# Retention and channel mix on one core: k transposed by whole 128x128 products, mu transposed on chip, and a rewritten order of all pieces

## The chip, the core and the metric

The kernel runs on one core of a Trainium2 chip. A core has TensorE (PE, the matrix engine; PEld is its weight load), VectorE (DVE), ScalarE (ACT), GpSimd (POOL) and SyncE (SP), each with its own instruction stream executed in order, and 16 DMA engines that they share. The metric is the device time of the program in microseconds, as the median of several runs.

## The reference

Per batch b and head h a state of 64x64 is decayed and updated at each of 768 tokens, read by q, and the result x goes through a channel mix with the token before it.

```python
# B=4, H=8, S=768, D=64;  d_model = 512, d_ff = 1024
gamma = 1 - 2.0 ** (-5.0 - arange(H));  scale = 1 / sqrt(D)
for t in range(S):
    state = gamma * state + k[t]^T v[t]            # per batch and head
    y[t]  = scale * q[t] @ state
x = y with heads side by side                      # (B, S, 512)
xk = mu_k * x + (1 - mu_k) * x_prev                # x_prev: the token before, zero at t = 0
xr = mu_r * x + (1 - mu_r) * x_prev
out = sigmoid(xr @ w_r) * (relu(xk @ w_k) ** 2 @ w_v)
```

## The kernel before

The work is cut into 12 blocks of 256 tokens (three for each batch, `more(n)` is false for the last of a batch). Inside a block the 256 tokens are two halves (u = 0, 1) of 128; each partition holds two neighbouring tokens (i = 0, 1), so that partitions 0 to 63 hold half 0 and 64 to 127 half 1. Head pairs (j, with hp = 0, 1 inside the pair) are processed by 64x64 products that use the array in four quarters.

All scheduling is by hand: the string `ORDER` (lines 16 to 63) lists all pieces, and each engine executes its own pieces in that order. A word such as `K.3.1@5` is a code, the block, further arguments, and the PSUM bank after the @. The codes are:

- `lk`, `lq`, `lv`: loads of k, q and v of a block. `lk.n` is issued by SP, `lk.n.2` by POOL; q and v by POOL. `wk`, `wr`, `wv`: weight loads by POOL. `mu`: the two mu vectors, by ACT.
- `ks`: `scale_k` (line 181), k times its decay, on DVE (`ks.n.0`) or POOL (`ks.n.1`).
- `T.n.0`, `T.n.1`: `trans` (line 195), transposes of q and of the scaled k on PE, 32 products of 64x64 each; both share two PSUM banks. `E.n.0`, `E.n.1`: `transed` (line 207), the copies to SBUF by ACT.
- `S`: `scores` (line 222, PE); `M`: `masked` (line 234, DVE). `C`: `state` (line 244, PE); `U`: `summed` (line 262, DVE); `G`: `decayed` (line 272, POOL). `I`: `inter` (line 278) and `Y`: `intra` (line 290), both PE. `D`: `yout` (line 310, DVE), which writes x transposed.
- `dx`: `differ` (line 318), x minus its predecessor, on DVE in blocks 0 and 1 and on POOL after that. `X.n.w.j.j+1`: `mixed` (line 325, DVE), xk for w = 0 and xr for w = 1, in four pieces each.
- `K`: `keys` (line 334, PE), four groups; `Q`: `squared` (line 344, ACT). `R`: `gate` (line 351, PE); `s`: `opened` (line 358, ACT). `V`: `values` (line 363, PE), in halves of the contraction; `O`: `result` (line 370, DVE); `st`: `store` (line 376, SP).
- `z.n`: `zeros` (line 397), n products of zeros on PE which nobody reads.

Attention pieces run ahead of the channel mix pieces by one or two blocks, and from the third block on the order interleaves them with K, R and V. The buffers are rings (`ring`): 4 for q, v and k as loaded, 3 for the scaled k.

Of the kernel before, what the change touches and what calls it, by code (L numbers as in the profile page):

```python
# [9 lines left out]
F16 = mybir.dt.float16  # L10
# [4 lines left out]
KSC = 64.0  # L15
ORDER = """
lk.0 lq.0 lv.0 gy lk.1.2 lq.1 lv.1 wk.0 ks.0.0 wk.1 z.13@0 T.0.0@01 wr T.0.1 lk.2.2 E.0.0 C.0@23
U.0.0 lq.2 E.0.1 z.1@4 I.0.0@45 U.0.1 G.0.1 z.2@6 S.0.0@01 mu S.0.1@23 lv.2 ks.1.0 z.2@7 T.1.0@67
wv.0 M.0.1 T.1.1 E.1.0 M.0.0 C.1@23 wv.1 E.1.1 U.1.0 Y.0 G.1.0 S.1.0@67 D.0 I.1.0@01 lk.3.2 M.1.0
z.2@2 S.1.1@45 M.1.1 lq.3 dx.0.0 Y.1 X.0.0.0.1 X.0.0.1.2 X.0.0.2.3 lv.3 X.0.0.3.4 X.0.1.0.1 z.9@2  # L20
K.0.0@2 X.0.1.1.2 X.0.1.2.3 K.0.2@4 X.0.1.3.4 lk.4.2 Q.0.0 U.1.1 D.1 R.0.0@5 ks.2.1 Q.0.2 T.2.0@23
R.0.1@4 s.0.0 lq.4 dx.1.0 T.2.1 s.0.1 K.0.1@5 E.2.0 lv.4 X.1.0.2.3 C.2@4 X.1.0.1.2 K.0.3@0 E.2.1
X.1.0.3.4 X.1.0.0.1 Q.0.1 X.1.1.0.1 S.2.0@23 K.1.0@1 G.1.1 M.2.0 Q.0.3 lq.5 V.0.0.0@5 U.2.0 Q.1.0
X.1.1.3.4 V.0.1.0@4 X.1.1.2.3 X.1.1.1.2 lk.5.2 V.0.1.1 G.2.0 V.0.0.1 O.0.1 ks.3.1 I.2.0@01 st.0.1
O.0.0 S.2.1@23 R.1.0@4 M.2.1 st.0.0 T.3.0@67 s.1.0 lv.5 T.3.1 lk.7 Y.2 E.3.0 lq.6 C.3@45 D.2
R.1.1@2 E.3.1 lv.6 K.1.1@3 U.3.0 s.1.1 ks.4.1 U.3.1 S.3.0@67 Q.1.1 I.3.0@45 S.3.1@01 M.3.0 K.1.2@2
G.3.1 lk.8 V.1.1.0@3 M.3.1 Q.1.2 dx.2.1 V.1.0.0@2 K.1.3@0 lk.6.2 X.2.0.3.4 C.4@67 Q.1.3 X.2.0.0.1
Y.3 X.2.0.1.2 lq.7 T.4.0@01 X.2.0.2.3 T.4.1 V.1.0.1 U.4.0 ks.5.1 E.4.0 D.3 V.1.1.1 E.4.1 O.1.0
K.2.0@6 G.4.0 O.1.1 st.1.0 lk.9 ks.7.1 S.4.0@01 U.4.1 Q.2.0 I.4.0@23 st.1.1 S.4.1@45 M.4.0 K.2.1@7
K.2.2@6 M.4.1 G.4.1 Q.2.1 lk.11 dx.3.1 K.2.3@7 Q.2.2 V.2.0.0@4 Q.2.3 V.2.1.0@5 lv.7 X.2.1.2.3  # L30
X.2.1.3.4 V.2.0.1 X.2.1.1.2 lq.8 X.3.1.0.1 X.3.0.0.1 V.2.1.1 X.2.1.0.1 X.3.0.2.3 R.2.0@7 X.3.0.3.4
X.3.0.1.2 R.2.1@6 X.3.1.1.2 s.2.0 X.3.1.2.3 T.5.0@01 X.3.1.3.4 s.2.1 T.5.1 O.2.0 ks.6.1 C.5@7
E.5.0 Y.4 U.5.0 st.2.0 O.2.1 R.3.0@4 E.5.1 D.4 st.2.1 G.5.0 K.3.0@5 lk.10 s.3.0 ks.8.1 S.5.0@23
Q.3.0 I.5.0@01 S.5.1@67 M.5.0 R.3.1@4 dx.4.1 K.3.1@5 M.5.1 s.3.1 K.3.2@4 Q.3.1 K.3.3@5 lv.8
X.4.0.0.1 Q.3.2 X.4.0.3.4 V.3.0.0@6 X.4.0.1.2 lq.9 X.4.0.2.3 Q.3.3 X.4.1.1.2 V.3.1.0@7 X.4.1.0.1
X.4.1.3.4 V.3.0.1 X.4.1.2.3 V.3.1.1 O.3.0 C.6@45 st.3.0 O.3.1 T.6.0@23 T.6.1 U.6.0 lq.10 Y.5
st.3.1 E.6.0 U.6.1 K.4.0@4 D.5 ks.9.1 E.6.1 R.4.0@5 Q.4.0 S.6.0@23 G.6.1 I.6.0@01 S.6.1@67 M.6.0
R.4.1@4 s.4.0 dx.5.1 K.4.1@5 M.6.1 s.4.1 K.4.2@4 Q.4.1 lv.9 X.5.0.2.3 X.5.0.1.2 K.4.3@5 X.5.0.0.1
Q.4.2 X.5.0.3.4 V.4.0.0@6 X.5.1.0.1 Q.4.3 X.5.1.1.2 V.4.1.0@7 X.5.1.2.3 X.5.1.3.4 V.4.0.1 V.4.1.1
O.4.0 T.7.0@45 st.4.0 O.4.1 T.7.1 lq.11 C.7@23 E.7.0 Y.6 st.4.1 U.7.0 K.5.0@7 G.7.0 D.6 E.7.1  # L40
ks.10.1 R.5.0@2 U.7.1 Q.5.0 S.7.0@45 I.7.0@67 S.7.1@01 M.7.0 s.5.0 K.5.1@3 G.7.1 dx.6.1 K.5.2@2
M.7.1 Q.5.1 K.5.3@3 Q.5.2 lv.10 X.6.0.0.1 V.5.0.0@0 X.6.0.1.2 Q.5.3 X.6.0.3.4 V.5.1.0@1 X.6.0.2.3
X.6.1.3.4 V.5.0.1 X.6.1.2.3 X.6.1.1.2 V.5.1.1 X.6.1.0.1 O.5.0 R.5.1@3 st.5.0 C.8@0 s.5.1 T.8.0@45
U.8.0 T.8.1 Y.7 O.5.1 G.8.0 E.8.0 R.6.0@0 ks.11.1 st.5.1 D.7 E.8.1 K.6.0@1 s.6.0 S.8.0@45 dx.7.1
Q.6.0 I.8.0@67 S.8.1@23 M.8.0 R.6.1@0 K.6.1@1 M.8.1 s.6.1 lv.11 K.6.2@0 Q.6.1 X.7.0.0.1 X.7.0.1.2
K.6.3@1 X.7.0.2.3 Q.6.2 X.7.0.3.4 V.6.0.0@2 X.7.1.0.1 X.7.1.2.3 Q.6.3 V.6.1.0@3 X.7.1.3.4
X.7.1.1.2 V.6.0.1 V.6.1.1 O.6.0 C.9@01 st.6.0 O.6.1 T.9.0@45 T.9.1 U.9.0 Y.8 st.6.1 E.9.0 U.9.1
K.7.0@0 D.8 G.9.1 E.9.1 R.7.0@1 dx.8.1 Q.7.0 S.9.0@45 I.9.0@67 S.9.1@23 M.9.0 R.7.1@0 s.7.0
K.7.1@1 M.9.1 s.7.1 K.7.3@0 Q.7.1 X.8.0.1.2 X.8.0.3.4 K.7.2@1 X.8.0.2.3 Q.7.3 X.8.0.0.1 V.7.0.0@2
X.8.1.1.2 Q.7.2 X.8.1.0.1 V.7.1.0@3 X.8.1.3.4 X.8.1.2.3 V.7.0.1 V.7.1.1 O.7.0 C.10@01 st.7.0 O.7.1  # L50
T.10.0@45 T.10.1 U.10.0 Y.9 st.7.1 E.10.0 G.10.0 K.8.1@0 D.9 E.10.1 R.8.0@3 U.10.1 dx.9.1 Q.8.1
S.10.0@45 I.10.0@67 S.10.1@01 M.10.0 K.8.0@2 s.8.0 G.10.1 R.8.1@3 M.10.1 Q.8.0 K.8.2@2 X.9.0.0.1
s.8.1 X.9.0.1.2 V.8.0.0@0 X.9.0.2.3 Q.8.2 X.9.0.3.4 V.8.1.0@1 X.9.1.0.1 X.9.1.1.2 K.8.3@2
X.9.1.2.3 X.9.1.3.4 C.11@3 Q.8.3 T.11.0@45 U.11.0 T.11.1 Y.10 G.11.0 E.11.0 V.8.0.1 D.10 E.11.1
V.8.1.1 O.8.0 dx.10.1 S.11.0@45 O.8.1 st.8.0 I.11.0@67 S.11.1@23 R.9.0@0 M.11.1 st.8.1 K.9.2@1
s.9.0 M.11.0 K.9.1@0 Q.9.2 X.10.0.0.1 R.9.1@1 X.10.0.1.2 Q.9.1 X.10.0.2.3 K.9.0@4 X.10.0.3.4
X.10.1.1.2 s.9.1 K.9.3@5 X.10.1.2.3 Q.9.0 X.10.1.3.4 X.10.1.0.1 Y.11 Q.9.3 V.9.0.0@4 D.11 V.9.0.1
dx.11.1 V.9.1.0@5 O.9.0 V.9.1.1 st.9.0 X.11.0.0.1 K.10.0@4 X.11.0.1.2 X.11.0.3.4 R.10.0@6
X.11.0.2.3 Q.10.0 X.11.1.0.1 K.10.1@4 X.11.1.3.4 s.10.0 X.11.1.1.2 K.10.2@7 X.11.1.2.3 Q.10.1
O.9.1 R.10.1@6 st.9.1 Q.10.2 V.10.0.0@5 s.10.1 V.10.1.0@4 K.10.3@6 R.11.0@7 Q.10.3 K.11.0@6 s.11.0  # L60
V.10.0.1 Q.11.0 V.10.1.1 O.10.0 R.11.1@6 st.10.0 O.10.1 K.11.1@7 st.10.1 s.11.1 K.11.2@6 Q.11.1
K.11.3@7 Q.11.2 V.11.1.0@4 Q.11.3 V.11.0.0@5 V.11.0.1 V.11.1.1 O.11.0 st.11.0 O.11.1 st.11.1
# [4 lines left out]
def kernel(  # L67
# [32 lines left out]
    gk_np = gam[None, :, None] ** (C - 1 - tok[:, None, :])  # L100
# [5 lines left out]
        [x.reshape(P, -1) for x in (gk_np, gd_np, g0_np, pw_np)], axis=1  # L106
# [15 lines left out]
    KS = ring("ks_", 3, [H, 2 * D], F16)  # L122
    QT = ring("qT_", 3, [2, NJ, C], F16)
    KT = ring("kT_", 3, [2, NJ, 2, D], F16)
# [11 lines left out]
    csm = const.tile([P, 2 * H + (2 + LOG) * NJ], F32, name="csm_sb")  # L136
    gy = const.tile([P, NJ, C], F32, name="gy_sb")
    zero = const.tile([P, 512], F16, name="zero")
    muk = const.tile([P, NCO], F32, name="muk")
    mur = const.tile([P, NCO], F32, name="mur")  # L140
# [7 lines left out]
    gk = csm[:, 0:o]  # L148
    gd = csm[:, o : o + NJ]
    g0 = csm[:, o + NJ : o + 2 * NJ]  # L150
    pw = csm[:, o + 2 * NJ :].rearrange("p (l j) -> p l j", l=LOG)
# [4 lines left out]
    relus = iter(range(NFO * NBLK))  # L156
# [24 lines left out]
    def scale_k(n, e, j0=0, j1=NJ):  # L181
        h0, h1 = 2 * j0, 2 * j1
        (nc.vector, nc.gpsimd)[e].tensor_tensor(  # L183
            out=KS(n)[:, h0:h1].rearrange("p h (i d) -> p (h i) d", i=2),
            in0=K32(n)[:, h0:h1].rearrange("p h (i d) -> p (h i) d", i=2),
            in1=gk[:, 2 * h0 : 2 * h1, None].to_broadcast([P, 2 * (h1 - h0), D]),
            op=ALU.mult,
        )

    def turned(n):  # L190
        return banks("T", n).bitcast(F16).rearrange(
            "p u (j a i t) -> p u j a i t", j=NJ, a=2, i=2
        )

    def trans(n, a, j0=0, j1=NJ):
        pt, src = turned(n), (Q16, KS)[a](n)
        for j in range(j0, j1):
            for i in range(2):
                for u in range(2):
                    r = slice(u * D, u * D + D)  # L200
                    for hp in range(2):
                        nc.tensor.transpose(  # L202
                            pt[hp * D : hp * D + D, u, j, a, i, :],
                            src[r, 2 * j + hp, i * D : i * D + D], ident[r, r],
                        )

    def transed(n, a, j0=0, j1=NJ):
        pt = turned(n)[:, :, j0:j1, a]
        if a == 0:
            t = QT(n)[:, :, j0:j1]  # L210
            nc.scalar.copy(  # L211
                out=t.rearrange("c u j (p i) -> c u j p i", i=2),
                in_=pt.rearrange("c u j i p -> c u j p i"),
            )
        else:
            t = KT(n)[:, :, j0:j1]
            nc.scalar.copy(
                out=t.rearrange("c u j i p -> c u j (i p)"),
                in_=pt.rearrange("c u j i p -> c u j (i p)"),
            )  # L220

    def scores(n, i):
        pa = pairs(banks("S", n, i))
        for j in range(NJ):
            for hp in range(2):
                r = slice(hp * D, hp * D + D)
                for u in range(2):
                    nc.tensor.matmul(  # L228
                        pa[u * D : u * D + D, hp, j, :], lhsT=KT(n)[r, u, j, i, :],
                        rhs=QT(n)[r, u, j, :],  # L230
                        start=(j == 0), stop=(j == NJ - 1), skip_group_check=True,
                    )
# [237 lines left out]
```

## Time and profile before

| what | value |
|---|---|
| median of 3 runs | 170.39 us (169.95 to 171.98) |
| the profiled execution's own time | 169.35 us |
| its span (first to last instruction) | 167.3 us |
| PE busy | 152.2 us, 91% of the span |
| PEld, DVE, ACT, POOL busy | 96.2, 120.3, 93.5, 78.2 us |
| instructions in the trace | 6065, of which 2717 matmuls and as many weight loads |

The profile comes from one execution. Its span is 2.05 us shorter than that execution's own time, which lies 1.04 us below the median. A busy time of PE counts matmuls that overlap each other as one stretch. "The chain that ended last" goes back from the last instruction to what released it; its rows are start, duration and what ran.

### The profile page before, as it was taken

Reading aid. Unit: us, or ns where it says so; the run is one execution under the profiler, and the core shown is the slowest. Engines: PE = TensorE matmul, PEld = TensorE weight load, DVE = VectorE, ACT = ScalarE, POOL = GpSimd, SP = SyncE. Lnnn points to the kernel's source line nnn. Section 1 sums busy time; section 2 is a strip of 40 time slices with the busy share of each in tenths; the row PEclk is TensorE's granted clock in tenths of the full one; section 3 lists DMA queues with packets and bytes.
Section 4 is the critical chain, followed back from the end, with each engine's and each line's share of the span. In section 5 each row is a group of like instructions: output and inputs, shape, how many; then the busy total and the mean of one; then the engine's idle time right before and its main releaser. Section 6 shows DMA issues by size and latency. Waiting matters only on the chain.

```text
span 167.3 us, 6065 instructions
## 1 busy us (share of the span) xinstructions
PE 152.2 (91%) x2717; PEld 96.2 (57%) x2717; DVE 120.3 (72%) x194; ACT 93.5 (56%) x146; POOL 78.2 (47%) x75
## 2 busy tenths in 40 slices
PE   7884799989498969999999999999999999999990
PEld 2344446647365826756747756676566767566640
DVE  2676999696586999877877967977678699670311
ACT  3133009918145826776658738937657649286660
POOL 7984369395956952926809609114024140400000
PEclk9999579999789999999999999999999999999999
DMA  4999999999999991796569271630030030101303
GB/s 129 244 198 195 255 195 215 244 235 277 239 211 237 291 212 45 222 113 149 59 63 175 28 117 67 67 125 4 0 127 8 4 129 0 58 24 48 125 0 125
DMA packets 39529, 22.01 MB, mean 132 GB/s; under 512 B 26832, under 2 KB 35664, under 8 KB 39504
## 3 DMA queue, kind: packets, MB, share of 16 engines
q0 software_dynamic: 28464, 12.06, 53.2%
q1 hardware_dynamic: 9696, 9.44, 18.0%
q10 hardware_dynamic: 1344, 0.13, 1.2%
q8 instruction: 21, 0.34, 0.9%
q14 instruction: 4, 0.03, 0.0%
HBM read 24.25 MB, written 6.29 MB: 182 GB/s over the span
## 4 chain that ended last, share of the span: by engine, by line
PE 75%; DVE 9%; issue 5%; DMA 4%; ACT 2%; POOL 2%; DVEq 0%; POOLq 0%
PE ps L339 23%; PE ps L365 20%; PE ps L353 13%; DVE xr L329 5%; PE ps L228 4%; DMA k<-in_k_dram 4%; PE ps L298 4%; PE ps L202 4%; DVE a L236 3%; PE ps L399 2%; PE ps L255 2%; PE ps L285 2%; ACT k L349 1%; ACT kr L346 1%; DVE os L371 1%
## 5 line engine op out<-in xcount | busy, mean ns | idle before, releaser
L339 PE MATMUL ps<-xk,wk 128*128 128x256 f16 x384 | 47.8, 276 | 0.0
L365 PE MATMUL ps<-wv,k 128*128 128x512 f16 x192 | 44.6, 382 | 0.2 <-ACT k L349 0.2
L346 ACT ACTIVATE kr<-ps 128x512 f32<-128x512 f32 x48 | 28.4, 592 | 28.9 <-PE ps L339 28.9
L339 PEld LDWEIGHTS <-wk 128*128 128x128 f16 x384 | 37.0, 99 | 9.4 <-issue 0.2
L236 DVE TENSOR_TENSOR a<-ps,c_sb 128x1024 f16<-128x1024 f32 x24 | 28.5, 1219 | 10.5 <-PE ps L228 9.8
L349 ACT ACTIVATE k<-kr 128x512 f16<-128x512 f32 x48 | 30.3, 631 | 1.5
L365 PEld LDWEIGHTS <-k 128*128 128x128 f16 x192 | 18.6, 99 | 20.7 <-ACT k L349 2.1
L371 DVE SCALAR_TENSOR_TENSOR os<-ps,rs 128x512 f32<-128x512 f32 x24 | 16.4, 688 | 19.1 <-PE ps L365 8.0
L273 POOL TENSOR_TENSOR tg<-t,csm_sb 128x256 f16<-128x256 f32 x16 | 10.1, 629 | 37.0 <-DVE t L270 31.7
L353 PE MATMUL ps<-wr,xr 128*128 128x512 f16 x96 | 24.6, 380 | 1.9 <-DVE xr L329 1.4
L329 DVE SCALAR_TENSOR_TENSOR xr<-dx,mur,xT 128x256 f16<-128x256 f32 x48 | 25.3, 584 | 0.0
L320 POOL TENSOR_TENSOR dx<-xT 128x1024 f32<-128x1024 f32 x10 | 18.9, 1891 | 10.1 <-DVE xT L312 10.1
L359 ACT ACTIVATE rs<-ps 128x512 f32<-128x512 f32 x24 | 14.2, 590 | 16.8 <-PE ps L353 16.8
L329 DVE SCALAR_TENSOR_TENSOR xk<-dx,muk,xT 128x256 f16<-128x256 f32 x48 | 22.7, 533 | 1.1 <-POOL dx L320 1.0
L211 ACT COPY qT<-ps 128x1024 f16<-128x1024 f16 x12 | 12.1, 1010 | 19.1 <-PE ps L202 19.0
L183 POOL TENSOR_TENSOR ks<-k,csm_sb 128x1024 f16<-128x1024 f32 x10 | 19.3, 1927 | 0.9 <-POOL tg L273 0.8
L312 DVE TENSOR_TENSOR xT<-ps,gy_sb 128x1024 f32<-128x1024 f32 x12 | 14.7, 1223 | 3.4 <-PE ps L298 2.5
L170 POOL DMA_DIRECT2D q<-in_q_dram x12 | 10.9, 912 | 11.9 <-PE ps L202 9.9
L353 PEld LDWEIGHTS <-xr 128*128 128x128 f16 x96 | 8.6, 97 | 9.7 <-DVE xr L329 1.9
L228 PE MATMUL ps<-qT,kT 64*64 64x128 f16 x384 | 11.7, 227 | 2.6 <-issue 2.4
L170 POOL DMA_DIRECT2D v<-in_v_dram x12 | 11.0, 917 | 3.9 <-DMA wr<-in_moe_w_r_dram 2.1
L228 PEld LDWEIGHTS <-kT 64*64 64x64 f16 x384 | 8.2, 108 | 7.7 <-issue 4.5
(32 smaller groups left out, 119.2 us busy)
## 6 DMA issues: line engine op xcount, KB each, us to landing
out_dram<-os SPq DMA_DIRECT2D x24, 256.0 KB, 3.1
k<-in_k_dram SPq DMA_DIRECT2D x6, 512.0 KB, 4.7
q<-in_q_dram POOLq DMA_DIRECT2D x12, 256.0 KB, 8.6
v<-in_v_dram POOLq DMA_DIRECT2D x12, 256.0 KB, 6.8
k<-in_k_dram POOLq DMA_DIRECT2D x6, 512.0 KB, 13.8
wk<-in_moe_w_k_dram POOLq DMA_DIRECT2D x2, 512.0 KB, 10.6
wv<-in_moe_w_v_dram POOLq DMA_DIRECT2D x2, 512.0 KB, 17.1
wr<-in_moe_w_r_dram POOLq DMA_DIRECT2D x1, 512.0 KB, 13.7
```

Of the source, the lines that this page charges most:

```text
L170: eng.dma_start(out=d(n)[:, 2 * j0 : 2 * j1], in_=rows(x, n)[:, 2 * j0 : 2 * j1])
L183: (nc.vector, nc.gpsimd)[e].tensor_tensor(out=KS(n)[:, h0:h1].rearrange("p h (i d) -> p (h i) d", i=2), in0=K32(n)[:, h0:h1].rearrange("p ...
L228: nc.tensor.matmul(pa[u * D : u * D + D, hp, j, :], lhsT=KT(n)[r, u, j, i, :], rhs=QT(n)[r, u, j, :], start=(j == 0), stop=(j == NJ - 1), ...
L236: nc.vector.tensor_tensor(out=t[:, i], in0=pairs(banks("S", n, i)), in1=causal[:, i, None, None, :].to_broadcast([P, 2, NJ, C]), op=ALU.mult,)
L320: (nc.vector, nc.gpsimd)[e].tensor_tensor(out=DX(n)[:, j0:j1], in0=x[:, j0:j1, c : c + TM], in1=x[:, j0:j1, c - 1 : c + TM - 1], op=ALU.su ...
L329: nc.vector.scalar_tensor_tensor(out=XM[w](n)[:, j], in0=DX(n)[:, j], scalar=mu[:, j : j + 1], in1=x[:, j, c - 1 : c + TM - 1], op0=ALU.mu ...
L339: nc.tensor.matmul(pz[:, i, :], lhsT=wk16[:, co, fo * P : fo * P + P], rhs=XM[0](n)[:, co, :], start=(i == 0 and co == 0), stop=(co == NCO ...
L346: nc.scalar.activation(out=kr, in_=banks("K", n, g).rearrange("p (i t) -> p i t", i=2), func=AF.Relu)
L349: nc.scalar.activation(out=K2(n)[:, 2 * g : 2 * g + 2], in_=kr, func=AF.Square)
L353: nc.tensor.matmul(banks("R", n, tb), lhsT=XM[1](n)[:, co, tb * P : tb * P + P], rhs=wr16[:, co, :], start=(co == 0), stop=(co == NCO - 1),)
L365: nc.tensor.matmul(banks("V", n, tb, 0), lhsT=K2(n)[:, fo, tb * P : tb * P + P], rhs=wv16[:, fo, :], start=(fo == 0), stop=(fo == NFO - 1),)
L371: nc.vector.scalar_tensor_tensor(out=OS(2 * n + tb), in0=banks("V", n, tb, 0), scalar=1.0 / (KSC * KSC), in1=RS(2 * n + tb), op0=ALU.mult, ...
```

## The change

- k is transposed by 8 products of 128x128 for each block, where there were 32 of 64x64. For this `KS` is laid out as (i, head, d), so that the two heads of a pair lie side by side; `scale_k` writes that layout, and `state` reads it. Each transpose of k has one PSUM bank of its own. q keeps its 32 products of 64x64, as the new piece `Tq` (`trans_q`), in two banks. `QT` and `KT` change their axes.
- mu is loaded as 8 rows of 128 values at the start, transposed by one PE product (`mt`) against a small identity that travels with `csmall`, and copied by ACT (`me`) to one tile `mu`.
- The second half of tokens of the last block (tile 11.1) is computed by column halves: `Vc`, `Oc`, `sc`, with the two stores on SP and on ACT.
- `ORDER` is rewritten throughout. All loads of k but the first are on POOL's queue; there were six on SP's. `ks.2` goes to DVE. There are 39 zero products instead of 29.
- Functions for halves of tokens (`yout_u`, `differ_u`, `mixed_u`, `keys_u`, `squared_u`) are added, and the new order does not call them.

The new order begins like this; then follow one stretch of its middle and its end (in the old order the pieces `I.1.0`, `S.1.1` and `Y.1` stood ahead of the first K):

```
lk.0 lq.0 mu lv.0 gy wk.0 lk.1.2 z.7@0 mt@0 lq.1 me wk.1 lv.1 ks.0.0 z.5@1 Tq.0@01 wr E.0.0
T.0.1@2 lk.2.2 C.0@45 E.0.1 lq.2 U.0.0 U.0.1 z.2@3 S.0.0@23 I.0.0@01 S.0.1@67 M.0.0 G.0.1 wv.0
M.0.1 z.9@4 Y.0 ks.1.0 lv.2 D.0 z.4@5 T.1.1@6 wv.1 Tq.1@23 E.1.1 dx.0.0 E.1.0 X.0.0.3.4 z.7@4
S.1.0@23 lk.3.2 X.0.0.2.3 X.0.0.1.2 X.0.0.0.1 X.0.1.2.3 z.4@7 C.1@67 lq.3 X.0.1.3.4 K.0.1@0
X.0.1.1.2 X.0.1.0.1 K.0.3@1 U.1.0 Q.0.1 M.1.0 G.1.0 K.0.2@0 Q.0.3 lv.3 U.1.1 I.1.0@45 S.1.1@23
G.1.1 R.0.0@1 Q.0.2 M.1.1 lk.4.2 K.0.0@0 s.0.0 ks.2.0 Y.1 Q.0.0 lq.4 Tq.2@23 D.1 T.2.1@0 E.2.0
R.0.1@1 E.2.1 dx.1.0 z.1@6 V.0.1.0@2 lv.4 s.0.1 X.1.0.0.1 X.1.0.3.4 S.2.0@01 V.0.0.0@3 X.1.0.1.2
lq.5 X.1.0.2.3 X.1.1.3.4 K.1.0@4 X.1.1.1.2 X.1.1.0.1 C.2@5 X.1.1.2.3 Q.1.0 K.1.2@7 U.2.0 M.2.0
...
X.4.1.3.4 Q.4.1 R.4.0@2 D.5 lv.9 V.4.0.0@3 s.4.0 dx.5.1 R.4.1@2 K.4.3@6 s.4.1 X.5.0.2.3 S.6.0@01
Q.4.3 X.5.0.3.4 C.6@45 V.4.1.0@2 X.5.0.0.1 X.5.0.1.2 X.5.1.2.3 K.5.0@6 X.5.1.3.4 U.6.0 ks.9.1
...
V.11.0.1 st.10.0 Vc.11.1.0@4 O.11.0 Vc.11.1.1@0 st.11.0 Oc.11.1.0 sc.11.1.0.0 Oc.11.1.1
sc.11.1.1.1
```

The core of the rest:

```diff
-    KS = ring("ks_", 3, [H, 2 * D], F16)
-    QT = ring("qT_", 3, [2, NJ, C], F16)
-    KT = ring("kT_", 3, [2, NJ, 2, D], F16)
+    KS = ring("ks_", 3, [2, H, D], F16)
+    QT = ring("qT_", 3, [NJ, 2, C], F16)
+    KT = ring("kT_", 3, [NJ, 2, C], F16)
...
-            out=KS(n)[:, h0:h1].rearrange("p h (i d) -> p (h i) d", i=2),
-            in0=K32(n)[:, h0:h1].rearrange("p h (i d) -> p (h i) d", i=2),
+            out=KS(n)[:, :, h0:h1],
+            in0=K32(n)[:, h0:h1].rearrange("p h (i d) -> p i h d", i=2),
...
     def trans(n, a, j0=0, j1=NJ):
-        pt, src = turned(n), (Q16, KS)[a](n)
+        pt = turned(n, a, j0).rearrange("p (j i t) -> p j i t", j=NJ, i=2)
         for j in range(j0, j1):
+            for i in range(2):
+                if a:
+                    nc.tensor.transpose(
+                        pt[:, j, i], KS(n)[:, i, 2 * j : 2 * j + 2].rearrange("p h d -> p (h d)"),
+                        ident,
+                    )
...
+    def trans_q(n):
+        pt = turned(n, 0)[:, :, 0 : 2 * NJ * D].rearrange("p u (j i t) -> p u j i t", j=NJ, i=2)
+        for j in range(NJ):
             for i in range(2):
                 for u in range(2):
                     r = slice(u * D, u * D + D)
                     for hp in range(2):
                         nc.tensor.transpose(
-                            pt[hp * D : hp * D + D, u, j, a, i, :],
-                            src[r, 2 * j + hp, i * D : i * D + D], ident[r, r],
+                            pt[hp * D : hp * D + D, u, j, i, :],
+                            Q16(n)[r, 2 * j + hp, i * D : i * D + D], ident[r, r],
                         )
...
+    def values_c(n, tb, c):
+        x = slice(c * dm // 2, (c + 1) * dm // 2)
+        for fo in range(NFO):
+            nc.tensor.matmul(
+                banks("Vc", n, tb, c)[:, x], lhsT=K2(n)[:, fo, tb * P : tb * P + P],
+                rhs=wv16[:, fo, x], start=(fo == 0), stop=(fo == NFO - 1), skip_group_check=True,
+            )
...
     def load_mu():
-        nc.scalar.dma_start(out=muk, in_=moe_mu_k.rearrange("(co ci) -> ci co", ci=P))
-        nc.scalar.dma_start(out=mur, in_=moe_mu_r.rearrange("(co ci) -> ci co", ci=P))
+        for w, x in enumerate((moe_mu_k, moe_mu_r)):
+            nc.scalar.dma_start(
+                out=mu8[w * NCO : (w + 1) * NCO], in_=x.rearrange("(co ci) -> co ci", ci=P)
+            )
+
+    def trans_mu():
+        nc.tensor.transpose(banks("mt")[:, 0 : 2 * NCO], mu8[0 : 2 * NCO], ident8)
+
+    def copy_mu():
+        nc.scalar.copy(out=mu, in_=banks("mt")[:, 0 : 2 * NCO])
```

## The prediction

> **What bounds the kernel now.** I read the page's busy times and slices first, then the chain in order of time, then the groups.
>
> ```profile
> span 167.3 us, 6065 instructions
> ...
> PE 152.2 (91%) x2717; PEld 96.2 (57%) x2717; DVE 120.3 (72%) x194; ACT 93.5 (56%) x146; POOL 78.2 (47%) x75
> ...
> PE   7884799989498969999999999999999999999990
> ...
> PEclk9999579999789999999999999999999999999999
> DMA  4999999999999991796569271630030030101303
> ...
> PE 75%; DVE 9%; issue 5%; DMA 4%; ACT 2%; POOL 2%; DVEq 0%; POOLq 0%
> ```
>
> PE is full from about 64 us to the end (98.4 of 99 us in the table by stage); the gaps lie in the first 64 us, where DMA is full too and the clock dips twice. So there are two separate questions: how much PE work there is, and what the first 64 us lose. The chain answers the second.
>
> ```profile
> 21.16 3.10 PE ps L399 x9
> 24.27 1.75 PE ps L339 x16
> ...
> 39.41 0.97 PE ps L353 x4
> 40.38 0.87 PE ps L339 x8
> ...
> 41.92 2.22 issue
> 44.14 0.53 PE ps L228 x10
> 44.67 1.82 PE ps L339 x8
> ...
> 62.73 1.90 PE ps L353 x8
> 64.62 0.64 PE ps L202 x64
> ...
> 76.22 0.58 PE ps L202 x64
> ```
>
> Four losses follow. (1) The first K starts at 24.1; its last `xk` piece had ended at 22.54, but nine zeros on a half clock (0.43 us each until 23.1) stood in front: 1.5 us. (2) 2.2 us of "issue" at 41.9. The stages that end at 13.1, 20.5, 41.9 and 50.75, where PE stalls, hold 447, 703, 1471 and 1727 matmuls and weight loads: each is a multiple of 256 less 65. The instruction queue moved 21 packets, 0.34 MB, so 16 KB each: PE waits for its next 256 instructions behind a full DMA. (3) After it the clock is halved from 43.6 to 47.0: eight K take 1.82 where 0.87 is usual, and the following V 2.12 for 1.73; with the S before, 1.5 us. (4) R of block 2 starts at 62.7, V had ended at 61.2:
>
> ```profile
> 57.11 4.77 DVE L329 SCALAR_TENSOR_TENSOR xr<-dx,mur,xT 128x256 f16<-128x256 f32 x4
> 58.87 1.92 POOL L183 TENSOR_TENSOR ks<-k,csm_sb 128x1024 f16<-128x1024 f32 x1
> ```
>
> Four `mixed` pieces usually take 1.67; one of these lasts 3.58, until 0.3 us after POOL's `ks` has ended. The two engines collide (M and D, which read PSUM, run through POOL's work unstretched).
>
> **PE work, part by part.** The groups:
>
> ```profile
> L339 PE MATMUL ps<-xk,wk 128*128 128x256 f16 x384 | 47.8, 276 | 0.0
> L365 PE MATMUL ps<-wv,k 128*128 128x512 f16 x192 | 44.6, 382 | 0.2 <-ACT k L349 0.2
> L202 PE MATMUL ps<-c_sb,ks 64*64 64x64 f16 x384 | 5.4, 195 | 0.1
> ```
>
> *Transposes of k.* 64 quarter products take 0.58 in the chain, so the 32 of k cost 0.29 per block. No 128x128 product with 128 columns exists in this trace. K (256 columns) advances by 0.109 us, V (512) by 0.216: 0.42 ns a column and 2 ns, so 128 columns give 55 ns: 0.44 for eight, if the weights keep up. Weight loads 128 wide come as close as 61 ns (three of K's in 0.22 us, each 0.10): 0.49. The Trainium skill ("TensorE: Matmul & The Clock Gate") speaks against the change twice: under "Back-to-back issue gap" it gives some 81 ns for a stream with 128 columns, so 0.65 a block; Part 4 gives some 275 ns for a transpose of this size, which in series would be 2.2 a block, +23 us in all. The second is excluded as a spacing: K also lasts 276 and the next starts 109 later. I take 61 ns, the nearest row: +0.2 a block; ends 55 and 81 ns (+0.15 and +0.36). Blocks 5 to 11, which decide below: +1.3.
>
> *Changes between whole array and quarters.* Entering S after K costs 0.35 where later S take 0.22; K or R after quarters takes 0.97 for 0.86. A run of quarter pieces so costs some 0.2. From K.2.0 to the end I count 16 such runs in the old order and 20 in the new: +0.8.
>
> *Fewer instructions.* 24 products and loads less in each block; they matter only for the fetches below. `ks` keeps its size (1.9 on POOL, 1.2 to 1.6 on DVE), and the copies by ACT stay 1.0 each: nothing.
>
> *The last tile.* Eight V of 216 ns become sixteen of 109: nothing. O on 256 columns instead of 512 saves 0.25 (row of `mixed`, 0.48, against 0.69), and the last store halves; the last two took from 163.8 to 165.8 to move: 0.3. Together −0.5; PE's end to the span's end goes from 4.1 to 3.5.
>
> *Queues.* Five more k loads on POOL are 5 x 0.92 = 4.6 us on an engine idle for 89 us; they come after block 6, when POOL waits for buffers. If POOL were late, `dx` would be, treated below.
>
> **The start, walked along the new order.** PE: seven zeros until 4.2, then `mt` waits for mu. ACT can issue mu at 3.2 to 4.0, behind the table load; the small loads took 2.7 (csmall) and 4.4 us (c16) to land. I take 6.3 (ends 5.7 and 8.4, the latter with c16's time). Five zeros on the half clock 2.1, Tq.0 0.5, E.0.0 and E.0.1 1.0 each with 0.5 to change engines: S.0 at 11.8, against 10.1 now; behind `mt` on PE stand Tq.0, T.0.1 and C.0, and ACT's copies and all of DVE's work on block 0 wait for those. The slow loads of mu that go cost nothing: `mur` landed at 8.1 + 10.3 = 18.4, ahead of the first X at 20.9. DVE from there: M twice 12.3 to 14.7, ks.1 to 16.2, D.0 17.4, dx 18.6, X.0.0 to 20.3: first K at 20.3, 3.8 earlier, because M.1.0 and M.1.1 (2.4) and the zeros are out of the way. DVE goes on: X.0.1 21.9, U and M of block 1 25.1, ks.2 26.5, D.1 27.7, dx 29.0, X.1.0 30.7. PE meanwhile does K.0, R.0, attention of 1 and 2 and half of V.0, without a gap, except that V needs `wv`: issued some 1 us later than now (11.4 + 17.1 to land): about 29.3, a wait of 0.8. K.1.0 at 31.5. The pieces up to K.2.0 sum to 16.0 (3.5 K.1, 1.7 R.1, 1.7 second half of V.0, 3.5 V.1, 5.6 attention with its changes between whole and quarters): K.2.0 at 47.5. Their inputs are ready: the longest chain, Y.2, D.2, dx.2, X.2.0, takes 5.9 and has 8.3 us of PE work beside it. The old order reaches K.2.0 at 53.5, having done C.4 and Y.3 (1.1) besides.
>
> *Fetches.* Counted along the new order, 256-instruction boundaries fall on S.1.0, Y.1, K.1.1, V.0.0.1, K.2.0 and Tq.5, 6.2 to 7.5 us apart by my times. The old ones that stalled were 4.7 to 6.9 apart; fetches took 6 to 9, the longest with two k loads on SP's queue under way, which the new order doesn't have. I allow 0.5 (ends 0 and 3.7).
>
> Here a rule and the trace differ. The same page, Part 1, drops the clock after an idle window of about 3.4 us. Here 2.2 us of stall, busy work before it, sufficed. By the rule a repeated stall costs 2.2; by the trace 2.2 + 1.5 = 3.7. I use the trace. The start has the same risk: if the clock is half during z.9 after S.0.1, these last 3.9 us instead of 1.9, and K comes 1.7 later.
>
> **The sum.** From K.2.0 to PE's end the old kernel took 163.2 − 53.5 = 109.7, with 1.8 of waits (1.4 at 61.2 to 62.7, 0.4 at 118 to 120): 107.9 of work. New: 107.9 + 1.1 + 1.3 + 0.8 = 111.1. The slack of later blocks, from Y.n to the first K.n, is 1 to 3 us beyond the 5.1 of D, dx and X, but near zero at block 5; I allow 0.9 of waits. 47.5 + 0.5 + 111.1 + 0.9 = 160.0, plus 3.5: a span of 163.5, against 167.3. With 2.05 to the run and 1.04 to the median: **166.6 us**, −2.2%. Two per cent, 167.0, is about what a measurement of this kernel tells from no change; the forecast is just past it.
>
> **Rivals.**
>
> *Forecast* (0.58; 0.50 below 167.0, 0.08 above). Own range 162.5 to 168: the low end has no fetch or later wait and 55 ns transposes.
>
> *The fetch stall stays* (0.22): DMA is as full as before in the first 45 us, and V.0 or C.4/Y.3 exhausts the supply. For: four of the old boundaries lost time. Against: quarter pieces are spread out more. One stall with its cold clock, less the 0.5 allowed: +3.2, 169.8.
>
> *The transposes run at the page's 81 ns* (0.09), so the change doesn't do on PE what it says: 20 ns x 8 x 10 blocks left: +1.6, 168.2. With the stall as well, 171.4.
>
> *DVE becomes the bound* (0.11), slower. Place: POOL takes `ks` straight after `dx`, while DVE runs X (ks.9.1 follows dx.5.1 with no load between; the old order kept later X at 3.25 us for eight). DVE has per block M 2.4, D 1.2, X 3.3, O 1.4, U 0.7, so 9.1 of the 11.5 us of PE. It decides once collisions exceed 2.4 a block. Two a block at 2 us each: 13.1, 1.6 over; eight blocks: +12.8, 179. Against: M, D and O are not stretched, and most `ks` stand after loads.
>
> So faster 0.50, same 0.08 + 0.22 + 0.09 = 0.39, slower 0.11. The range 162.5 to 171.5 takes in the stall with slow transposes, and leaves out the bound by DVE and some of the low end.
>
> **What would show it.** Right: first K at 20 to 22 us; K of block 2 at 46 to 49; eight k transposes in about 0.5 in the chain; no "issue" over 1 us after 25 us; the last O about 0.4. Wrong: `mt` after 7 us with S.0 past 13; a clock dip between 25 and 64; X above 4 us per block after 64 us with PE waiting for `xk` or `xr`; PE's work from K.2.0 above 113.

## The result, and the profile after

The changed kernel took 169.7 us (median of 20 runs, 166.75 to 171.57), the kernel before 170.62 (median of 20). The ratio of the compared runs is **0.9855**, 95% interval 0.9815 to 0.9894: 1.5% faster, inside the two per cent that were called no change. The two medians lie only 0.5% apart, because the ratio leaves out runs that are over 1.5% above the fastest of the same kernel, and 12 of the changed kernel's 20 are such. A second set of runs, first in the experiments below, gives 0.9897 (0.9838 to 0.9956).

The lines below come from the profiled execution of the second set, whose span is 167.5 us and whose own time, 169.26 us, is close to the median; the one of the first set (span 169.7 us) is called the first profiled execution where it is used. First the page, with the rows that were shown of before:

```profile
span 167.5 us, 5527 instructions
...
PE 155.1 (93%) x2448; PEld 99.1 (59%) x2448; DVE 123.0 (73%) x196; ACT 93.9 (56%) x147; POOL 82.5 (49%) x79
...
PE   7699999999869949999969999999999999999992
...
PEclk9999999999969999999999999999999999999999
...
PE 79%; DVE 9%; issue 4%; DMA 2%; POOL 2%; ACT 2%; ACTq 1%; DVEq 0%; POOLq 0%
```

There are 269 fewer matmuls and as many fewer loads, yet PE is busy for longer. The start is now dense. The gaps have moved into slices 11, 12 and 15 (42 to 50 and 59 to 63 us) and slice 21 (84 to 88), and the one clock dip lies in slice 12. Then the chain of waits (start, duration, what ran):

```profile
18.69 0.97 PE ps L480 x4
19.66 0.38 PE ps L268 x32
20.03 2.73 PE ps L392 x24
...
30.21 0.87 PE ps L392 x8
...
42.09 1.19 DVE xk L355 x4
43.27 3.45 issue
46.72 0.69 DVE os L424
47.41 0.04 issue
47.45 3.54 PE ps L392 x16
...
58.86 1.74 DVE xk L355 x2
60.60 1.49 issue
62.09 0.84 DVE xk L355
62.93 0.04 issue
62.97 2.90 PE ps L392 x24
...
92.78 0.50 PE ps L201 x8
```

L392 is K, L355 the mixed pieces, L480 the zeros and L201 the transposes of k. The first K starts at 20.0 us instead of 24.1. K of block 1 starts at 30.2. From the first K until 40 us PE has no gap. Then K of block 2 and K of block 3 wait for xk, at 47.45 and at 62.97; the "issue" in front of each is time in which DVE held a mixed piece. The sixteen K after 47.45 take 3.54 us where 1.75 is usual: the clock was halved from 47.5 to 50.9 us. No wait for instructions is left on PE.

The waits of PE in the same trace:

```profile
PE ps L392 <- DVE xk L355: 3.8, 2, 2.4
PE ps L392 <- DVE os L424: 2.0, 1, 2.0
PE ps L473 <- DMA mu<-in_moe_mu_r_dram: 1.7, 1, 1.7
```

The second row names O because the wait lists several semaphores; the mixed piece ahead of O on DVE is what is late. The third is `mt`, as forecast. What DVE and POOL do there is seen in the timeline of each, from 42 us:

```profile
42.01 4.79 DVE L355 SCALAR_TENSOR_TENSOR xk<-dx,mu,xT 128x256 f16<-128x256 f32 x4
...
49.38 4.45 DVE L355 SCALAR_TENSOR_TENSOR xr<-dx,mu,xT 128x256 f16<-128x256 f32 x4
...
58.24 5.07 DVE L355 SCALAR_TENSOR_TENSOR xk<-dx,mu,xT 128x256 f16<-128x256 f32 x4
```

```profile
42.79 1.79 POOL L173 DMA_DIRECT2D k<-in_k_dram  x2
44.57 1.94 POOL L186 TENSOR_TENSOR ks<-k,csm_sb 128x1024 f16<-128x1024 f32 x1
...
50.42 1.94 POOL L186 TENSOR_TENSOR ks<-k,csm_sb 128x1024 f16<-128x1024 f32 x1
...
59.93 1.94 POOL L186 TENSOR_TENSOR ks<-k,csm_sb 128x1024 f16<-128x1024 f32 x1
```

Three times four mixed pieces take 4.5 to 5.1 us where 1.67 is usual, and each time one `ks` of POOL lies in the middle; the longest single pieces take 3.61, 3.27 and 2.58 us where 0.47 is usual. In the kernel before this happened too, but only its last case cost PE more than a microsecond.

So the working theory was: the new order gains some 4 us at the start and loses it to three or four collisions on the path to K and R (theory A). Its rivals: DVE has too much work in these stages anyway (B), or POOL's loads hold the mixed pieces, not `ks` (C). A second question came up by itself: what the 128x128 transposes do alone.

### The profile page after: what moved, and what is told of

It is laid out like the page before. It is cut to its first block, busy times and chain, and to the rows that moved or that the text cites. A ratio compares the mean times of both kernels' runs of the same rounds, so it can differ in the third digit from the quotient of the medians.

```text
span 169.7 us, 5527 instructions
## 1 busy us (share of the span) xinstructions
PE 155.1 (91%) x2448; PEld 99.0 (58%) x2448; DVE 123.3 (73%) x196; ACT 94.3 (56%) x147; POOL 82.7 (49%) x79
## 4 chain that ended last, share of the span: by engine, by line
PE 76%; DVE 13%; issue 3%; DMA 2%; POOL 2%; ACT 2%; ACTq 1%; DVEq 0%; POOLq 0%
PE ps L392 22%; PE ps L418 19%; PE ps L406 12%; DVE xk L355 6%; PE ps L480 5%; PE ps L243 4%; PE ps L299 3%; PE ps L312 3%; PE ps L201 3%; DVE xr L355 2%; DMA mu<-in_moe_mu_r_dram 2%; PE ps L219 2%; DVE a L250 2%; DVE os L424 2%; PE ps L268 1%
## 5 line engine op out<-in xcount | busy, mean ns | idle before, releaser
L392 PE MATMUL ps<-xk,wk 128*128 128x256 f16 x384 | 48.4, 278 | 6.5 <-DVE xk L355 3.8
L392 PEld LDWEIGHTS <-wk 128*128 128x128 f16 x384 | 37.4, 100 | 16.4 <-issue 7.4
L250 DVE TENSOR_TENSOR a<-ps,c_sb 128x1024 f16<-128x1024 f32 x24 | 29.1, 1219 | 11.3 <-PE ps L243 11.3
L355 DVE SCALAR_TENSOR_TENSOR xk<-dx,mu,xT 128x256 f16<-128x256 f32 x48 | 28.8, 660 | 9.0 <-POOL dx L341 8.9
L402 ACT ACTIVATE k<-kr 128x512 f16<-128x512 f32 x48 | 30.2, 630 | 1.5
L418 PEld LDWEIGHTS <-k 128*128 128x128 f16 x184 | 17.0, 98 | 18.0 <-issue 0.3
L341 POOL TENSOR_TENSOR dx<-xT 128x1024 f32<-128x1024 f32 x10 | 18.9, 1894 | 14.6 <-DVE xT L326 14.5
L424 DVE SCALAR_TENSOR_TENSOR os<-ps,rs 128x512 f32<-128x512 f32 x23 | 15.7, 686 | 11.3 <-ACT rs L412 6.4
L186 POOL TENSOR_TENSOR ks<-k,csm_sb 128x1024 f16<-128x1024 f32 x9 | 18.1, 2015 | 11.7 <-PE ps L268 11.7
L355 DVE SCALAR_TENSOR_TENSOR xr<-dx,mu,xT 128x256 f16<-128x256 f32 x48 | 23.6, 543 | 0.0
L287 POOL TENSOR_TENSOR tg<-t,csm_sb 128x256 f16<-128x256 f32 x16 | 10.7, 669 | 24.3 <-DVE t L284 24.3
L235 ACT COPY kT<-ps 128x1024 f16<-128x1024 f16 x12 | 12.2, 1012 | 10.5 <-PE ps L201 5.3
L173 POOL DMA_DIRECT2D v<-in_v_dram x12 | 11.1, 921 | 10.2 <-PE ps L312 4.4
L480 PE MATMUL ps<-zero 128*128 128x512 f16 x39 | 12.3, 457 | 1.2 <-DVE xT L464 1.2
```

The lines of the kernel that those rows point to most:

```text
L173: eng.dma_start(out=d(n)[:, 2 * j0 : 2 * j1], in_=rows(x, n)[:, 2 * j0 : 2 * j1])
L235: nc.scalar.copy(out=out, in_=pt)
L250: nc.vector.tensor_tensor(out=A2(n)[:, i, :, j0:j1], in0=pairs(banks("S", n, i, j0))[:, :, j0:j1], in1=causal[:, i, None, None, :].to_broa ...
L341: (nc.vector, nc.gpsimd)[e].tensor_tensor(out=DX(n)[:, j0:j1, t0:t1], in0=x[:, j0:j1, c + t0 : c + t1], in1=x[:, j0:j1, c - 1 + t0 : c - 1 ...
L355: nc.vector.scalar_tensor_tensor(out=XM[w](n)[:, j, t0:t1], in0=DX(n)[:, j, t0:t1], scalar=mu[:, w * NCO + j : w * NCO + j + 1], in1=x[:, ...
L392: nc.tensor.matmul(pz[:, i, :], lhsT=wk16[:, co, fo * P : fo * P + P], rhs=XM[0](n)[:, co, :], start=(i == 0 and co == 0), stop=(co == NCO ...
```

## The experiments

All ratios are to the kernel before, run beside it on the same chip; intervals are 95%.

**The changed kernel again** (e1).

> The changed kernel once more, as the yardstick on the same chip for the runs beside it. Ratio to the kernel before 0.98 to 0.99. If the collisions of POOL with mixed are what takes the lead away, then again: first K at 20.4 us, K of block 2 at 48, and mixed pieces of 2 to 3.5 us each between 42 and 64 us, with some 6 us of PE waits there. If the waits between 42 and 64 were a disturbance of one execution, they are absent here and the span is below 164.

0.9897 (0.9838 to 0.9956), with the trace shown above. The collisions came again at the same places; they are no accident of one execution.

**ks on DVE** (e2). Four words of the order change:

```diff
-ks.5.1  ks.6.1  ks.7.1  ks.9.1
+ks.5.0  ks.6.0  ks.7.0  ks.9.0
```

> The changed kernel with ks of blocks 5, 6, 7 and 9 on DVE instead of POOL, where the order has them. Theory A (POOL's ks, run straight after dx and its loads, holds DVE's mixed pieces, which K and R of blocks 2 to 5 wait for): each ks costs DVE 1.22 and frees it of 2 to 3 us; mixed pieces of xk and xr fall from 52 us busy to 44 to 46, PE waits from 40 to 64 us from 6 to about 2, no clock dip near 65; span 4 to 6 us shorter, ratio to the kernel before 0.955 to 0.965. Theory B (DVE simply has too much work in these stages, the collisions fill time in which it would wait anyway): 4.9 us more of DVE work, PE waits stay at 5 or more, ratio 0.98 to 1.0. Theory C (POOL's DMA issues hold mixed, not ks): the piece that starts at 42.8 stays at 2.2 us with no ks near it, ratio 0.975 to 0.985.

0.9531 (0.9487 to 0.9575), span 160.6 us. DVE's timeline of this kernel at the same places:

```profile
42.08 1.67 DVE L355 SCALAR_TENSOR_TENSOR xk<-dx,mu,xT 128x256 f16<-128x256 f32 x4
43.66 0.68 DVE L424 SCALAR_TENSOR_TENSOR os<-ps,rs 128x512 f32<-128x512 f32 x1
44.27 0.41 DVE L284 TENSOR_TENSOR t<-ps,tg 128x256 f32<-128x256 f32 x1
44.60 1.22 DVE L250 TENSOR_TENSOR a<-ps,c_sb 128x1024 f16<-128x1024 f32 x1
45.73 1.22 DVE L186 TENSOR_TENSOR ks<-k,csm_sb 128x1024 f16<-128x1024 f32 x1
```

Theory A holds in the main. The four mixed pieces take 1.67 again, `ks` takes 1.22 on DVE, and DVE as a whole is *less* busy with the added work (116.6 us against 123.0), which ends B. The clock is never halved between 10 and 160 us. PE's waits after 40 us are 1.2 us in all, and the ratio is slightly below the range that A gave. POOL still issues its loads of q and of k beside these pieces, and they are not stretched, so loads alone are not the cause either (C):

```profile
41.95 0.92 POOL L173 DMA_DIRECT2D q<-in_q_dram  x1
42.87 1.78 POOL L173 DMA_DIRECT2D k<-in_k_dram  x2
```

Loads are not without any part, though. In this trace one mixed piece, at 66.3 us, takes 0.84 us where 0.47 is usual, with nothing but two loads on POOL beside it. And in the first profiled execution of the changed kernel one piece was held for 2.18 us, from 42.80 us on, beside loads, and was let go as `ks` began (44.97). With no `ks` behind the loads, 0.4 us is the most that any piece lost here.

**The 128x128 transposes alone, in the old order** (e3). `scale_k`, `trans`, `transed`, `scores` and `state` use the new layouts for k; q, mu, the order and the tail are those of before. The two transposes still share two banks, q in the first half of each and k in the second.

> The kernel before, with its own order, in which k alone is transposed by eight 128x128 products (both transposes still in the shared two banks). By the forecast's sum: 0.45 to 0.5 instead of 0.29 a block and one more change between whole array and quarters (0.2), so 12 x 0.36 to 0.4 = 4.3 to 4.9 us of PE work, of which blocks 0 and 1 are hidden at the start: +3.5 to +4, less the fetch stall at 41.9 with its cold clock (up to 3.7) if fewer instructions remove it: ratio 1.0 to 1.023. If fewer instructions are worth more than the array time, the ratio is below 0.99.

0.9683 (0.9612 to 0.9755): three per cent *faster*, where the array's own cost had been expected to win. The array cost is there: from K.2.0 to PE's end this trace takes 48.6 to 158.6 = 110.0 us against 53.3 to 163.2 = 109.9 before. PE is busy for 109.8 of them against 107.9, so the work has grown by 1.8 us over the seven blocks that are transposed there. What outweighs it lies ahead of K.2.0, which comes 4.7 us earlier (1.9 of it already at the first K). The larger part is seen in the chain between 33 and 50 us:

```profile
39.81 0.87 PE ps L344 x8
40.68 0.35 PE ps L233 x16
...
41.24 0.22 PE ps L233 x10
41.47 0.98 PE ps L344 x8
42.45 1.73 PE ps L370 x8
```

The 2.22 us of "issue" at 41.9 are gone, and with them the half clock: K and V behind it run at 0.87 to 0.98 and 1.73. Only 1.0 us of waiting for instructions is left, at 14.4.

**The instruction count put back** (e5). The same kernel, with 24 of the old transposes in front of the new ones, which overwrite them:

```diff
     def trans(n, a):
         pt = turned(n, a)
+        for j in range(3 if a else 0):
+            for i in range(2):
+                for u in range(2):
+                    r = slice(u * D, u * D + D)
+                    for hp in range(2):
+                        nc.tensor.transpose(
+                            pt[hp * D : hp * D + D, u, j % 2, i, 0:D],
+                            KS(n)[r, i, 2 * j + hp], ident[r, r],
+                        )
```

> The kernel before with 128x128 transposes of k (as in the run of that alone, 0.968), and 24 of the old 64x64 transposes in front of them in every block, which the real ones overwrite: the instruction count of the kernel before is back (32 products for k and their loads), the array pays 24 x 9 ns = 0.22 us a block, and nothing else changes. If it was the number of instructions that removed the wait for PE's instructions near 41.9 us and the half clock behind it, both come back: 2.6 us of array plus 2 to 4, ratio 0.99 to 1.015. If the gain had another cause (layout of ks and kT, shorter copies, fewer mode changes), only the array time returns: ratio 0.978 to 0.986.

1.0182 (1.012 to 1.0245), slightly above the range that was expected. The gain is gone and more. The chain of this kernel has the stall back, and the stage that ends at it holds the same number of instructions as in the kernel before, 735 matmuls and 736 loads:

```profile
44.69 0.11 PE ps L242 x2
44.80 2.79 issue
47.59 0.53 PE ps L242 x10
48.12 1.82 PE ps L353 x8
```

```profile
0.00:44.85 44.85, 38.72 (x735) 22.56 (x736) 32.51 (x53) 17.82 (x26) 29.12 (x35) 0.89 1.39 216
```

(The second fence is a row of the table by stage: its time, then busy time and count of PE, PEld, DVE, ACT and POOL.) Between 0.9683 and 1.0182 lie only these 24 products a block. Their array time, 0.22 us each block, is 2.6 of the 8.5 us between the medians (165.66 and 174.13). The larger part is waiting for instructions (4.7 us in its list of waits, against 1.0), the half clock behind it (K and V 1.3 us longer), and a wait of 1.4 us for block 2's xr that returns with it. With the array time that is 9.0 of the 11.3 us by which the two profiled executions differ. Much of the rest lies in the start: after the first stop the half clock lasts from 16.4 to 26.6 us here, from 15.3 to 18.7 in e3.

The tables by stage also show why the stop goes away in e3. In the kernel before PE runs through the 256 instructions ahead of the stop in 3.8 us (38.1 to 41.9). In e3 the same 256 by count take 6.1 us (39.8 to 45.9), and PE crosses that boundary, the 1471st instruction, without a stop. From 76.1 to 79.4 us the kernel before needs only 3.3 us for 256 and does not stop either; there the DMA share in the table is 0.62, against 1.41 ahead of the stop. So the number of PE instructions was a bound of the kernel before, in the stage where DMA is full.

**k loads moved from SP to POOL, in the old order** (e4).

```diff
-lk.7  lk.8  lk.9  lk.10  lk.11
+lk.7.2  lk.8.2  lk.9.2  lk.10.2  lk.11.2
```

> The kernel before, in which the five k loads that SP issues behind stores (blocks 7 to 11) are issued by POOL at the same places of the order. If these loads make PE's instruction fetch at 1471 instructions late (two of them are under way from 37.8 us), the 2.2 us of issue at 41.9 and the half clock from 43.6 to 47 go: 2 to 3.7 us less, ratio 0.978 to 0.99. If the fetch waits behind POOL's own loads, the stall stays at 1.5 us or more and the ratio is 0.995 to 1.01; more loads beside mixed on POOL could add a collision of 1 to 2 us.

1.0 (0.997 to 1.0031). The stall stays at 2.46 us, at 42.75, with the half clock behind it. That SP issues these loads is not what makes the fetch late.

**ks on DVE in the kernel before** (e8): `ks.3.1`, `ks.5.1`, `ks.6.1` to `.0`.

> The kernel before with ks of blocks 3, 5 and 6 on DVE, the ones that stretch mixed pieces there (2.1, 2.2 and 3.6 us near 34, 46 and 57). Its waits for mixed pieces: 0.7 near 36 and 1.4 near 62; the wait for instructions at 41.9 with its half clock stays, since nothing about the instructions changes. Ratio 0.985 to 0.992. If it comes near 0.96, the collisions and not the instructions were the loss of the kernel before; if it stays at 0.995 or more, the time is taken by the next wait.

0.9873 (0.9813 to 0.9932), as expected. The waits for mixed pieces are gone, and 2.0 us of waiting for instructions at 43.2 with its half clock stays.

**Both in the old order** (e6): the transposes alone, plus `ks.3` and `ks.6` on DVE.

> The old order with 128x128 transposes of k, and ks of blocks 3 and 6 on DVE, the two that stretched mixed pieces in the run without this (2.1 us each near 33 and 55). If collisions cost the end time only where PE waits for a mixed piece, little is to be had: PE waited 0.8 us for it there; ratio 0.962 to 0.969. If the new order is worth nothing but what the collisions take, this equals the changed kernel with ks on DVE: 0.953. A clearly higher value says that the new order itself (first K 3.8 us earlier, last tile by columns) brings the rest.

0.9642 (0.9585 to 0.9699), not separable from the transposes alone. So four kernels stand beside each other. In the old order the transposes bring about 3% and the collisions little more. In the new order the collisions alone are worth 3.7 points (0.9897 to 0.9531, measured side by side). The new order without them is better than the old one by about one per cent (0.9531 against 0.9642; from two sets of runs, and the intervals just miss each other). No run has the old transposes in the new order, so what they bring there is not measured.

**mu later** (e7): the kernel of e2, with `mt` and `me` behind the first state product.

```diff
-lk.0 lq.0 mu lv.0 gy wk.0 lk.1.2 z.7@0 mt@0 lq.1 me wk.1 lv.1 ks.0.0 z.5@1 Tq.0@01 ...
+lk.0 lq.0 mu lv.0 gy wk.0 lk.1.2 lq.1 wk.1 lv.1 ks.0.0 z.12@0 Tq.0@01 ...
-T.0.1@2 lk.2.2 C.0@45 E.0.1 lq.2 ...
+T.0.1@2 lk.2.2 C.0@45 E.0.1 mt@7 me lq.2 ...
```

> The changed kernel with ks of blocks 5, 6, 7 and 9 on DVE (0.953), and the product that transposes mu moved behind the first state product, its copy behind the first copies, with the 12 zero products of the start in one piece. The forecast's claim: PE's wait for mu delays everything to the first K. If so: q's transposes at 6.8 instead of 8.6 us, first K at 18.4 to 19 instead of 20.1, ratio 0.943 to 0.949, unless the next limit takes it back: the loads of wv, which land at about 28 us, where the first V is now, would then hold V.0 and the gain would be 0 to 0.7 us, ratio 0.949 to 0.953.

0.9449 (0.9409 to 0.949), 161.71 us: the best version, ahead of both kernels. The first K starts at 18.9 instead of 20.0. Of these 1.1 us the span keeps 0.7 (159.9 against 160.6 in e2); the chain now goes through the weight loads, as the second half of the expectation had it, with a wait of 0.3 us:

```profile
11.12 15.76 DMA wv<-in_moe_w_v_dram
26.87 0.14 issue
27.01 1.02 PE ps L418 x4
```

## Why the prediction was right, and where it was not

The forecast was 166.6 us, −2.2%; measured was −1.5%, in the stated range, but on the other side of the two per cent. That it came so near is in part luck. Without the collisions (e2) the span is 160.6 us, 2.9 shorter than the 163.5 that were forecast, and the collisions add 6.9. Step by step:

- *The start.* First K forecast at 20.3, measured 20.0 and 20.4 in the two traces. `mt` at 6.3, measured 6.0 and 6.5. K of block 1 at 31.5, measured 30.2: the 0.8 us for `wv` was not needed. This part is right, and e7 shows that the named price of `mt` is real: 1.1 us at the first K, and 0.7 us of span (the intervals of the ratios of e2 and e7 just meet).
- *K of block 2* at 47.5 plus 0.5; measured 47.45. That is partly luck. Without collisions (e2) it is 45.4: the pieces from K.1.0 summed to 15.1 us, not 16.0, and the 0.5 for fetches was nothing. The 2.0 us wait for xk made up for it.
- *Work from there to PE's end.* 111.1 of work and 0.9 of waits, so 112.0. In e2, where the collisions are gone, it took 45.4 to 157.3 = 112.0, with 1.2 us of waits, so 110.8 of work: the sum of pieces was right to half a microsecond, the transposes included. Eight take 0.45 to 0.55 us in the chain, the 0.55 where they follow quarter products, so near the 55 ns end. The 81 ns that the Trainium skill gives for such a stream ("TensorE: Matmul & The Clock Gate", "Back-to-back issue gap"; the rival of chance 0.09) are excluded here: inside one group the transposes start 56 ns apart. (Seven blocks at +0.2 are 1.4, not the 1.3 that went into the sum.) In the changed kernel itself the stretch took 47.45 to 164.26 = 116.8.
- *The step that failed is "I allow 0.9 of waits".* It measured about 5.8: 2.4 us for block 3's xk, 1.8 by the half clock after block 2's wait, 1.4 at block 5, 0.2 near 100. The 4.9 us too little here and the 2.0 for the wait in front of K.2.0, less the 2.6 us too much before it and the 0.3 too much for the tail, are the 4 us between the forecast span (163.5) and that of this execution. The mechanism was named, as the rival with DVE as the bound, with block 5 as its place (right: 3.32 for four pieces, near 82). Two things in it were wrong. It asked for collisions on all blocks before they matter, because it compared DVE's sum with PE's; in fact three collisions suffice where K or R stands next. And it took "most `ks` stand after loads" as protection. The loads end while the mixed pieces are still under way, and `ks` meets them.
- *Fetches.* "They matter only for the fetches below" named the right place and put too little on it. The boundaries of the new order fall where the forecast counted them, 6.2 to 9.0 us apart, and no fetch stall was left (0.5 allowed); in the old order that absence is most of what the transposes bring (e3 against e5). One reading was wrong: the boundary ahead of the stop at 41.9 was crossed 3.8 us before it, not 4.7 to 6.9. The cause offered for the long fetch, k loads on SP's queue, is refuted by e4.
- *The tail.* PE's end to the span's end: 3.2 us, forecast 3.5.
- *The rule on the clock.* The 2.0 us of waiting in front of K.2.0 were followed by a half clock of 3.4 us. That is one of the signs of being wrong that the forecast named, a clock dip between 25 and 64 us. So a wait shorter than the 3.4 us of idling that the Trainium skill gives ("TensorE: Matmul & The Clock Gate", Part 1) can halve the clock, as the trace of before had shown. But its length alone does not decide. In the same trace the 2.4 us in front of block 3's K were followed by no half clock. In the first profiled execution it was the other way about: 2.2 us up to 48.1 without one, 2.4 us up to 63.6 with one, from 64.7 to 68.1. What decides is not shown here, so "2.2 + 1.5" is what a stall can cost, not what it must.

What stays open: a held mixed piece can start to wait before `ks` begins by the record (43.19 us against 44.57, with loads of k between), and one was let go as `ks` began. In e2 the same loads, with no `ks` behind them, held none of these pieces. How a `ks` that stands behind loads acts before its recorded start is not shown; no run tells it apart.

## What to carry to other kernels

Count the instructions of a matrix engine as work of their own while DMA is full: a form that costs the array more (0.45 for 0.29 us) can win by fetching a quarter of the instructions, and the multiples of 256 at the stalls show whether that is so. Before an order is judged by sums of engine time, look at which element-wise pieces from SBUF to SBUF run on DVE while POOL has one of its own, and whether PE waits for them next; four words of the order were worth more here (3.7 points) than the rest of the rewriting (about one). A change that "does little" can be one large gain and one large loss: this one holds about 5% of gain and gave most of it back.

## What the runs showed of the hardware

- PE's instructions come in blocks of 256: the instruction queue moved 21 packets for the 5434 products and loads of the kernel before, and 19 for the 4858 of e3. PE stopped at the same instruction (735 matmuls and 736 loads) at 41.9, 42.75, 43.2 and 44.8 us in four kernels with the same instruction count (before, e4, e8, e5), for 2.0 to 2.8 us; with 24 fewer products a block it did not stop there.
- One `ks` on POOL (1.9 us) holds a mixed piece on DVE for 2 to 3.6 us, while DVE can do the same `ks` in 1.22. Pieces that read PSUM (M, D, O) were not held. Beside loads alone a piece lost at most 0.4 us (e2).
- A wait of 2.0 us after busy work was followed by 3.4 us of half clock on PE, at a cost of 1.8 us; another of 2.4 us in the same trace was not.
- 128x128 transposes of 128 columns start 56 ns apart inside a group of eight, which takes 0.45 to 0.55 us in the chain, against 9 ns for one in quarters of 64x64, of which four times as many are needed.
